# Where a head's sums get their start value, how the hashes are multiplied, and a list of jobs in another order

## The chip, the cores and the metric

The kernel runs on one core of one Trainium2 chip. The metric is the device time of one execution in microseconds (us); the lower the better. The core has a matrix engine (TensorE, PE in the profile, with its weight loads as PEld), VectorE (DVE), ScalarE (ACT), GpSimd (POOL) and SyncE (SP), each with a queue of its own that it works through in order, and 16 DMA engines that move data.

## What is computed

Attention over 4 batches of 8 heads, 768 tokens and 64 dimensions, in which a query sees only the keys of its own hash bucket, and behind it a layer that sends the 128 best tokens of a batch through a small network.

```python
q_bits = (einsum(q, proj) > 0)                 # 6 bits a token: its bucket; k_bits alike
mask   = q_bucket[..., :, None] == k_bucket[..., None, :]
scores = where(mask, q @ k.T / 8, -1e9)
attn   = softmax(scores)                       # sum + 1e-9 below
x      = (attn @ v) as (B, 768, 512)
# per batch: the 128 tokens with the highest x . w_gate
ye  = relu(xe @ w1) @ w2                       # 512 -> 1024 -> 512
out[top] = x[top] + sigmoid(x[top] . w_gate) * ye      # the other tokens keep x
```

## The kernel before

**The program is a list of words.** `ORDER` holds some 2,000 words such as `s.6.4`; `jobs` gives each its function, and the words are emitted one after the other. So each engine's queue is the list, filtered by engine: what stands ahead of an instruction on its engine has to be done first. `BANKS` deals the PSUM tiles (`big` 1024 columns, `one` 512) in the order in which they are asked for. The sums of a head have a PSUM bank of their own, the pool `pav` with one buffer, so that a head's sums can start only when those of the head before have been read.

**A head (0 to 31, eight to a batch) goes through these words.**
- `X` loads it (queries and keys transposed, float32), `xh` and `xl` split it into two float16 tiles XH and XL on ScalarE and GpSimd. `h` (line 342) multiplies four heads by the projection `pjt`, each in 32 columns of the array of its own (`tile_position`), `sg` takes the signs. `pa`, `pb`, `ps` are DMAs on SyncE's queue that put the parts into the operands A and B. Head 0 goes a shorter way (`hx`, `sx`, `da`, `dd`).
- `mx`, `re`, `rd` (lines 499, 507, 515): the largest bucket-matched score of a query, by differences of keys in three passes that ScalarE clamps between; `mt`, `mc`, `mr` (520, 524, 530) turn these maxima into a row and store it into A.
- `s.h.u` (565, 568): the scores in five units; `e` (581) the exponentials on ScalarE; `r` (595) their low halves on VectorE.
- `w` (606): the start value of the sums. It is what all the keys together give a query without a match: two products of 396 columns for each head, of a constant with `W`, which GpSimd makes from the sums of v (`vs`, `vw`).
- `a.h.c` (621): probabilities times values, 18 products of 64 or 65 columns for each of six chunks of keys. `rc` (631 to 633) and `n` (641) divide on VectorE; `po` stores.

**A batch** then scores its tokens (`sc`, `sl`), ranks them (`lt`, `ow`, counted by `cl`, `cw` on TensorE), makes the list (`se`, `ip`, `ix`), gathers the tokens (`ga`, GpSimd), and runs the network: `tx`, `hi`, `lo`, `up.b.f` (872, twelve products of 128 columns for each of eight f), `hh` and `hl` (the two halves of the hidden layer, ScalarE and VectorE), `dn.b.f` (903), `fi`, `sr` (scatter). For batches 0 to 2 this lies among the heads of the next batches; for batch 3 nothing comes behind it, and that is the tail of the program.

The lines that the steps turn on: `seed` 599 to 609, `hash_` 338 to 346, `load_pj` 252, `max_turn` 517 to 520, `finish` 907, `scatter` 914, and `ORDER`.

Of the kernel before, what the change touches and what calls it, by code (L numbers as in the profile page):

```python
# [45 lines left out]
w.0 pa.3.0 re.2.0.0 mx.1.0.2 pa.3.1 xl.2 re.2.1.0 rd.1.0 X.7 mx.2.0.1 xh.4 pb.1.2 mx.2.1.1 pb.1.3 re.2.0.1 vs.1 rd.1.1
rt.0 pa.4.0 re.2.1.1 X.6 rk.0.1 mx.2.0.2 rk.0.0 pb.2.3 ia.3 mt.1 mx.2.1.2 xh.5 rd.2.0 pb.2.2 s.0.0 pb.3.0 V.3 mc.1
pb.3.1 e.0.0 rd.2.1 s.0.2 mr.1 s.0.4 pa.4.1 e.0.2 mt.2 s.0.3 mc.2 vw.1 mr.2 s.0.1 e.0.3 r.0.0 ps.3.0 h.1.0.4 e.0.1
ia.4 ps.3.1 pb.4.0 e.0.4 a.0.0 sg.1.0.4 pa.5.0 a.0.1 pb.4.1 s.1.0 pa.5.1 ps.5.0 s.1.1 e.1.0 kd.3 ps.5.1 s.1.2 r.0.1
ps.4.0 e.1.1 mx.3.0.0 r.0.2 ps.4.1 mx.3.1.0 a.0.2 e.1.2 vs.2 a.0.3 re.3.0.0 a.0.4 a.0.5 r.1.0 re.3.1.0 s.1.3 rc.0 vs.3  # L50
# [922 lines left out]
```

## Time and profile before

| | us |
|---|---|
| median of 3 runs (lowest, highest) | 428.82 (427.92, 429.24) |
| the profiled execution's own time | 429.79 |
| its span, first to last instruction | 428.0 |
| busy in the span: TensorE | 388.4 |
| VectorE | 297.2 |
| ScalarE | 289.9 |
| GpSimd | 159.7 |

The profiled execution took 1.8 us more than its span, and 0.97 us more than the median. An engine's busy time counts each instant once, however many instructions overlap in it. TensorE's instructions overlap heavily: what one costs is read from the distance of two starts, not from its length.

### The profile page before, as it was taken

How to read it: one execution, taken by the hardware profiler on the slowest of the kernel's cores; microseconds unless marked ns; L12 is line 12 of the kernel's file. 1: busy time of each engine (PE TensorE's matmuls, PEld its weight loads, DVE VectorE, ACT ScalarE, POOL GpSimd, SP SyncE). 2: the span in 40 equal slices, each digit the busy share in tenths (PEclk: the TensorE clock that was granted, in tenths of full speed). 3: DMA queues.
4: the chain of work that ended last, by engine and by line, in shares of the span. 5: the costliest groups of instructions: out<-in, count | busy, mean ns of one | idle time of the engine just before them, and what ended most of it. 6: DMA issues, size and time to landing. Idle time of an engine off the chain costs nothing.

```text
span 428.0 us, 13488 instructions
## 1 busy us (share of the span) xinstructions
PE 388.4 (91%) x5633; PEld 291.0 (68%) x5640; DVE 297.2 (69%) x628; ACT 289.9 (68%) x367; POOL 159.7 (37%) x172
## 2 busy tenths in 40 slices
PE   0699999999989799999999999999999999999375
PEld 0255877777767577887667786887667777877272
DVE  1656767778786799767677978865859788467511
ACT  2677799698869877677857968678746877552010
POOL 9379668373726245414314150423141212000100
PEclk9759999999999999999999999999999999999679
DMA  8676268756484665514464257323343223001100
GB/s 242 195 192 160 63 182 252 242 167 165 107 289 88 157 176 184 159 53 124 110 190 142 66 149 229 86 59 99 105 128 96 64 61 100 2 3 71 54 2 25
DMA packets 33685, 53.87 MB, mean 126 GB/s; under 512 B 5726, under 2 KB 24920, under 8 KB 33624
## 3 DMA queue, kind: packets, MB, share of 16 engines
q1 hardware_dynamic: 22440, 33.48, 29.0%
q10 hardware_dynamic: 10544, 17.43, 12.9%
q0 software_dynamic: 640, 2.10, 1.6%
q8 instruction: 44, 0.72, 0.8%
q14 instruction: 17, 0.14, 0.1%
HBM read 25.78 MB, written 7.35 MB: 77 GB/s over the span
## 4 chain that ended last, share of the span: by engine, by line
PE 60%; DMA 12%; DVE 11%; issue 7%; SPq 5%; ACT 3%; ACTq 0%; POOL 0%; POOLq 0%; DVEq 0%
PE av L621 17%; PE mx L499 11%; PE s L565 10%; PE s L568 10%; DMA A<-XH 4%; PE hp L872 4%; DMA A<-sg 3%; PE yp L903 2%; DVE R L595 2%; PE av L606 2%; PE h L342 2%; DMA pjt<-in_pj_dram 2%; ACT mx L507 1%; DMA X<-in_qk_dram 1%; SPq L402 1%
## 5 line engine op out<-in xcount | busy, mean ns | idle before, releaser
L581 ACT ACTIVATE P<-s 128x1024 int32<-128x1024 f32 (+1 forms) x160 | 146.6, 938 | 45.8 <-PE s L568 43.2
L565 PE MATMUL s<-A 97*128 97x512 f16 (+1 forms) x384 | 118.3, 326 | 3.2 <-DVE mr L524 2.1
L507 ACT ACTIVATE mx<-mx 128x512 f32<-128x512 f32 (+2 forms) x127 | 100.2, 801 | 29.5 <-PE mx L499 23.7
L621 PEld LDWEIGHTS <-P 128*128 128x128 f16 x2304 | 114.6, 97 | 6.4 <-issue 0.6
L568 PE MATMUL s<-B 128*128 128x512 f16 (+1 forms) x384 | 118.0, 326 | 0.0
L621 PE MATMUL av<-V,P 128*128 128x65 f16 (+1 forms) x2304 | 118.0, 193 | 0.0
L621 PE MATMUL av<-VR,R 128*128 128x65 f16 x1152 | 114.6, 192 | 1.1 <-DVE R L595 1.1
L595 DVE TENSOR_SCALAR R<-P 128x1536 f16<-128x1536 uint16 x96 | 97.7, 1029 | 15.6 <-ACT P L581 15.5
L621 PEld LDWEIGHTS <-R 128*128 128x128 f16 x1152 | 105.2, 98 | 1.5 <-DVE R L595 1.5
L373 POOL TENSOR_TENSOR XL<-X,XH 128x768 f16<-128x768 f32 x32 | 53.5, 1677 | 86.3 <-DVE R L595 18.3
L515 DVE TENSOR_REDUCE m<-mx 128x2 f32<-128x512 f32 (+1 forms) x65 | 61.5, 951 | 20.0 <-PE mx L499 18.2
L499 PEld LDWEIGHTS <-A 96*128 96x128 f16 x570 | 53.6, 100 | 31.3 <-issue 12.2
L499 PE MATMUL mx<-kd,A 96*128 96x256 f16 (+1 forms) x378 | 63.0, 284 | 6.4 <-DVE kd L473 3.6
L568 PEld LDWEIGHTS <-B 128*128 128x128 f16 x384 | 37.6, 98 | 22.5 <-issue 3.9
L565 PEld LDWEIGHTS <-A 97*128 97x128 f16 x384 | 37.4, 97 | 19.3 <-issue 0.8
L499 PE MATMUL mx<-A 96*128 96x256 f16 (+1 forms) x192 | 33.2, 284 | 1.2 <-ACT mx L507 1.2
L444 POOL TENSOR_TENSOR vs<-Vf 128x384 f32<-128x384 f32 x16 | 17.9, 1122 | 42.2 <-DMA Vf<-in_v_dram 42.1
L915 POOL DMA_INDIRECT out_dram<-ye,idx x4 | 5.6, 1404 | 71.8 <-DVE ye L910 65.3
L362 ACT CAST XH<-X 128x768 f16<-128x768 f32 x32 | 26.5, 830 | 8.4 <-DMA A<-XH 5.9
L872 PE MATMUL hp<-xth,w1h 128*128 128x128 f16 x128 | 24.4, 229 | 2.3 <-DVE htl L890 0.9
L872 PE MATMUL hp<-xtl,w1h 128*128 128x128 f16 x128 | 24.3, 229 | 0.5 <-DVE ss L857 0.5
L473 DVE TENSOR_TENSOR kd<-A 96x512 f16<-96x512 f16 (+1 forms) x32 | 15.0, 471 | 14.0 <-PE mx L499 9.1
(97 smaller groups left out, 453.1 us busy)
## 6 DMA issues: line engine op xcount, KB each, us to landing
X<-in_qk_dram SPq DMA_DIRECT2D x30, 384.0 KB
Vf<-in_v_dram ACTq DMA_DIRECT2D x16, 384.0 KB
B<-A SPq DMA_DIRECT2D x64, 96.0 KB
B<-XL SPq DMA_DIRECT2D x64, 96.0 KB
out_dram<-x ACTq DMA_DIRECT2D x8, 768.0 KB
A<-XH SPq DMA_DIRECT2D x62, 96.0 KB
wt<-in_w_dram ACTq DMA_DIRECT2D x8, 512.0 KB
sbc<-scores SPq DMA_DIRECT2D x3, 384.0 KB
```

Of the source, the lines that this page charges most:

```text
L362: nc.scalar.copy(xh, st["X", h])
L373: turn(nc.gpsimd.tensor_tensor(**rest_x(h)))
L444: nc.gpsimd.tensor_tensor(y, t[:, 0:3], t[:, 3:6], op=ALU.add)
L499: nc.tensor.matmul(p[:, t - t0], a[0:96, 0, t * P : (t + 1) * P], keys, start=first, stop=True, skip_group_check=True,)
L507: nc.scalar.activation(p, p, AF.Relu)
L515: nc.vector.reduce_max(st["m", h][:, t0:t1], max_tile(h, g), axis=AX.X)
L565: nc.tensor.matmul(p[:, o : o + n], a[:, 1, c * P : (c + 1) * P], a[:, 0, q0 : q0 + n], start=True, stop=False,)
L568: nc.tensor.matmul(p[:, o : o + n], bt[:, 1, c * P : (c + 1) * P], bt[:, 0, q0 : q0 + n], start=False, stop=True,)
L581: nc.scalar.activation(pp[:, c0 : c0 + k, q0 : q0 + w], p[:, : k * w].rearrange("p (c q) -> p c q", c=k), AF.Exp, bias=PB * float(np.log(2 ...
L595: mine(nc.vector.tensor_scalar(r, pp.bitcast(U16)[:, :, 0::2], 2.0 ** -24, None, op0=ALU.mult,))
L621: nc.tensor.matmul(o[:, t, 0:n], l, r, start=False, stop=last and l is lo, skip_group_check=True,)
L872: nc.tensor.matmul(o, l[:, k, fs], st[r, b][:, xs], start=(f % 4 == 0 and k == 0 and i == 0), stop=(k == 3 and i == 2), skip_group_check=True,
```

## The change

- **The start value of the sums.** For each pair of heads TensorE makes one small product (`ws`, twice 132 columns), ScalarE copies it to SBUF (`wc`), and for each head ScalarE copies it, six times side by side, into the PSUM bank of the sums (`w`, 396 columns), in place of the two products of 396 columns. At the very start one product with zeros (`zb`) clears the bank.
- **The hash** of groups 1 to 7 is made from float16 pairs: projection high times XH, high times XL, low times XH, 24 products of 384 columns in place of 8 in float32. It then waits for XL, where it waited for X. `pp` makes the two halves of the projection.
- **The maxima** are clamped and rounded to float16 first (`mq`, VectorE), then turned in float16 (`mt`), then copied (`mc`).
- **The start.** The projection is loaded second on SyncE's queue, the other constants, the gate and the first weights later; the constant rows of A are written by VectorE and GpSimd in pieces; 30 products of a constant (`wu.0.30`) run ahead of the first hash; ScalarE's table is loaded by `it`.
- **The list.** It is made anew. All eight `up.2` now stand behind the last head's sums, with `dn.2`, `fi.2` and the scatter behind them; the scatter of batch 2 stands behind the gather of batch 3.
- **Buffers.** X 4 in place of 5, XH and XL 6 in place of 3; the rank's mask and the list's mask share a buffer; `fi` writes over its input.

```diff
 def seed(h):                                   # before; after: seed_act
-    for i in range(2):
-        nc.tensor.matmul(st["O", h], zs, w[:, i, h % 2].unsqueeze(1).broadcast_to([P, NC, OW]),
-                         start=(i == 0), stop=False, skip_group_check=True)
+def out_clear():
+    o = out_tile(0)
+    nc.tensor.matmul(o[:, : NC * OW], zs, zero, start=True, stop=True, skip_group_check=True)
+def sum_all(pr):
+    for i in range(2):
+        nc.tensor.matmul(
+            p[:, : 2 * OW], zs, W[pr % NV][:, i].rearrange("p h d -> p (h d)"), start=(i == 0), stop=(i == 1)
+        )
+def sum_copy(pr):
+    nc.scalar.copy(t.rearrange("p h d -> p (h d)"), st["wp", pr][:, : 2 * OW])
+def seed_args(h):
+    if h:
+        out_tile(h)
+    return st["O", h], st["W", h // 2][:, h % 2].unsqueeze(1).broadcast_to([P, NC, OW])
+def seed_act(h):
+    nc.scalar.copy(*seed_args(h))
...
 def hash_(g, j0, j1):
+        if g:
+            need(("pj",))
+            terms = ((pjh, "XH"), (pjh, "XL"), (pjl, "XH"))
+        else:
+            terms = ((pjt[:, 0:32], "X"),)
         for e in range(2):
-            for j in range(j0, j1):
-                nc.tensor.matmul(hp[32 * j : 32 * j + 32, ...], pjt[:, 0:32], st["X", 4 * g + j][...],
-                    start=True, stop=True, tile_position=(0, 32 * j))
+            for i, (w, x) in enumerate(terms):
+                for j in range(j0, j1):
+                    nc.tensor.matmul(hp[32 * j : 32 * j + 32, ...], w, st[x, 4 * g + j][...],
+                        start=(i == 0), stop=(i == len(terms) - 1), tile_position=(0, 32 * j))
...
+def max_clamp(h):
+    m = st["mq", h] = sb.tile([P, NC], F16, tag="mq", name=f"mq{h}", bufs=2)
+    nc.vector.tensor_scalar(m, st["m", h], FLOOR, 1.0 / MS, op0=ALU.max, op1=ALU.mult)
 def max_turn(h):
-    nc.tensor.transpose(out=p[:NC, :P], in_=st["m", h], identity=ident)
+    nc.tensor.transpose(out=p[:NC, :P], in_=st["mq", h], identity=ident16)
 def max_copy(h):
-    nc.vector.tensor_scalar(mr, st["mt", h][:NC, :P], FLOOR, 1.0 / MS, op0=ALU.max, op1=ALU.mult)
+    nc.vector.tensor_copy(mr, st["mt", h][:NC, :P])
...
 ORDER, behind the last head's products (two pieces):
-a.31.5 sc.3.1.3 dn.2.0 rc.31 dn.2.1 sl dn.2.2 n.31 dn.2.3 bp.0 po.7 dn.2.4 bc.0 bp.1 dn.2.5 ow.3.0 bc.1
+a.31.5 up.2.0 rc.31 up.2.4 sl up.2.5 n.31 up.2.1 po.7 bp.0 bp.1 bc.0 up.2.2 bc.1 ow.3.0 up.2.3 lt.3.0
```

How the instructions stand in the two programs follows at three places, as a listing of each queue prints it; a name's digits up to the underscore are its batch or head and part, those behind it only number the tile.

SyncE's queue at the start of the program, before (X0 and X1 are the first two heads, cs and c16 constants, pjt the projection):

```order
L298 DMA X0_96<-in_qk_dram 64x768
L298 DMA X1_103<-in_qk_dram 64x768
L256 DMA cs_67<-in_cst_dram 128x259
L253 DMA pjt_69<-in_pj_dram 128x96
L301 DMA X2_113<-in_qk_dram 128x768
L301 DMA X3_120<-in_qk_dram 128x768
```

And of the change:

```order
L321 DMA X0_103<-in_qk_dram 64x768
L262 DMA pjt_69<-in_pj_dram 128x99
L321 DMA X1_111<-in_qk_dram 64x768
L268 DMA c16_68<-in_cst16_dram 128x262
L324 DMA X3_120<-in_qk_dram 128x768
L324 DMA X2_155<-in_qk_dram 128x768
L432 DMA B0_87<-A0_82 64x768 x2
L422 DMA A1_83<-XH1_186 64x768 x2
```

The projection moved from the fourth place to the second, the float32 constants left this stretch.

TensorE at the seed of head 3 before: the last unit of its scores and the first of the two products of 396 columns, which stands there twice (zs is the constant, W1 the sums of v):

```order
L565 LDWEIGHTS A3_82
L565 MATMUL s3_4_1027<-A3_82 128x256
L568 LDWEIGHTS B3_87
L568 MATMUL s3_4_1027<-B3_87 128x256
L606 LDWEIGHTS zs_73
L606 MATMUL av3_1036<-W1_93,zs_73 128x396
```

And of the change ScalarE's queue around a seed, that of head 6 (P are exponentials, mx clamps, wp the small product, V a split of v, av the sums):

```order
L609 ACTIVATE P6_1_1803<-s6_3_1749 128x2x512
L537 ACTIVATE mx8_0_1739<-mx8_0_1739 128x1024
L647 COPY ws4_1846<-wp4_1830 128x132
L453 ACTIVATE V0_91<-Vf4_1115 128x12x64
L537 ACTIVATE mx8_1_1717<-mx8_1_1717 128x512
L656 COPY av6_1865<-ws3_1249 128x396
L609 ACTIVATE P6_1_1803<-s6_4_1835 128x2x256
L609 ACTIVATE P7_0_1890<-s7_0_1855 128x2x512
```

The start value left TensorE's queue and stands in ScalarE's, among instructions that wait for TensorE.

VectorE in the tail before, from the copy of the scores to the rank (co and cm are comparisons, ye the end of batch 2):

```order
L740 SCALAR_TENSOR_TENSOR co3_7799<-sbc3_7783,sc2_7771,cs_67 128x128
L703 COPY sbc3_7783<-bp_7784 128x384
L740 SCALAR_TENSOR_TENSOR co3_7799<-sbc3_7783,sc2_7771,cs_67 128x128 x2
L729 TENSOR_SCALAR cm3_0_7807,acc_74<-sbc3_7783,sc2_7771 128x640
L729 TENSOR_SCALAR cm3_2_7812,acc_74<-sbc3_7783,sc2_7771 128x384
L740 SCALAR_TENSOR_TENSOR co3_7799<-sbc3_7783,sc2_7771,cs_67 128x128
L910 SCALAR_TENSOR_TENSOR ye2_7821<-yp2_7759,ss2_7038,xe2_6954 128x512
L729 TENSOR_SCALAR cm3_1_7824,acc_74<-sbc3_7783,sc2_7771 128x512
L740 SCALAR_TENSOR_TENSOR co3_7799<-sbc3_7783,sc2_7771,cs_67 128x128 x2
L729 TENSOR_SCALAR cm3_4_7838,acc_74<-sbc3_7783,sc2_7771 128x128
L729 TENSOR_SCALAR cm3_3_7840,acc_74<-sbc3_7783,sc2_7771 128x256
L767 TENSOR_TENSOR rank3_7848<-rp3_7815,acc_74 128x6
```

And of the change:

```order
L753 COPY sbc3_7977<-bp_7978 128x384
L790 SCALAR_TENSOR_TENSOR co3_7999<-sbc3_7977,sc2_7946,cs_67 128x128
L779 TENSOR_SCALAR cm3_0_8013,acc_77<-sbc3_7977,sc2_7946 128x640
L779 TENSOR_SCALAR cm3_1_8015,acc_77<-sbc3_7977,sc2_7946 128x512
L790 SCALAR_TENSOR_TENSOR co3_7999<-sbc3_7977,sc2_7946,cs_67 128x128 x4
L779 TENSOR_SCALAR cm3_2_8060,acc_77<-sbc3_7977,sc2_7946 128x384
L779 TENSOR_SCALAR cm3_3_8062,acc_77<-sbc3_7977,sc2_7946 128x256
L790 SCALAR_TENSOR_TENSOR co3_7999<-sbc3_7977,sc2_7946,cs_67 128x128
L940 SCALAR_TENSOR_TENSOR htl2_8030<-hp2_7916,hth2_8029 128x512
L779 TENSOR_SCALAR cm3_4_8074,acc_77<-sbc3_7977,sc2_7946 128x128
L940 SCALAR_TENSOR_TENSOR htl2_8030<-hp2_7916,hth2_8029 128x512
L817 TENSOR_TENSOR rank3_8087<-rp3_8034,acc_77 128x6
```

Two instructions for the low half of batch 2's hidden layer (htl2) now stand ahead of the rank, and the end of batch 2 went behind it.

## Rows read from the trace of the kernel before

**Rows 1.** the page, busy time, share of the span and instructions of each engine

```profile
PE 388.4 (91%) x5633; PEld 291.0 (68%) x5640; DVE 297.2 (69%) x628; ACT 289.9 (68%) x367; POOL 159.7 (37%) x172
```

**Rows 2.** stretches of the span: length, busy time by engine, clock, DMA share, GB/s

```profile
0.00:32.60 32.60, 17.97 (x77) 9.09 (x78) 15.27 (x21) 18.09 (x24) 22.55 (x42) 0.79 0.72 210
32.60:157.00 124.40, 118.42 (x1774) 88.81 (x1774) 93.61 (x173) 104.10 (x130) 70.65 (x64) 1.00 0.60 167
157.00:390.20 233.20, 229.59 (x3606) 178.18 (x3609) 175.31 (x394) 165.31 (x210) 63.50 (x64) 1.00 0.38 106
390.20:428.00 37.80, 22.45 (x181) 14.92 (x179) 12.99 (x42) 2.36 (x5) 2.96 (x3) 0.80 0.12 42
```

**Rows 3.** timeline of TensorE near 164 us: start, length, engine, line, tiles, count

```profile
163.88 1.50 PE L342 MATMUL h<-X,pjt 128*32 128x384 f32 x16
165.31 0.39 PE L565 MATMUL s<-A 97*128 97x512 f16 x1
...
166.19 0.50 PE L606 MATMUL av<-W,zs 128*128 128x396 f16 x2
166.52 0.82 PE L499 MATMUL mx<-kd,A 96*128 96x256 f16 x6
```

**Rows 4.** timeline of TensorE near 94 us and 377 us, same columns

```profile
94.20 0.27 PE L520 MATMUL mt<-cs,m 128*6 128x128 f32 x1
94.30 0.60 PE L499 MATMUL mx<-kd,A 96*128 96x256 f16 x4
...
376.90 0.22 PE L872 MATMUL hp<-xth,w1h 128*128 128x128 f16 x1
...
377.57 0.50 PE L606 MATMUL av<-W,zs 128*128 128x396 f16 x2
```

**Rows 5.** groups of instructions by line and shape: busy us, mean ns | idle before

```profile
L507 ACT ACTIVATE mx<-mx 128x1024 f32<-128x1024 f32 x62 | 62.8, 1014 | 16.0 <-PE mx L499 13.5 <-DVE V L429 1.5 <-ACT XH L362 0.3
...
L342 PEld LDWEIGHTS h<-X,pjt 128*32 128x32 f32 x124 | 4.4, 111 | 15.1 <-issue 14.5 <-DMA X<-in_qk_dram 0.3
...
L703 ACT COPY sbc<-bp 128x384 f32<-128x384 f32 x1 | 0.5, 479 | 5.1 <-PE bp L696 5.1
```

**Rows 6.** timeline of VectorE behind a head's last product

```profile
163.98 0.17 DVE L631 TENSOR_SCALAR rc<-av 128x6 f32<-128x6 f32 x1 [0.21 <-PE av L621]
...
164.61 0.56 DVE L641 TENSOR_TENSOR x<-av,rc 128x384 f32<-128x384 f32 x1
```

**Rows 7.** timeline of the first 33 us, all engines

```profile
4.79 2.09 DVE L336 CAST A<-X 32x768 f16<-32x768 f32 x2 [4.79 <-DMA X<-in_qk_dram]
...
9.70 0.82 PE L342 MATMUL h<-X,pjt 128*32 128x384 f32 x1 [9.70 <-DMA pjt<-in_pj_dram]
...
18.28 1.44 PE L499 MATMUL mx<-kd,A 96*128 96x384 f16 x4 [3.63 <-DVE kd L473]
...
32.61 0.38 PE L565 MATMUL s<-A 97*128 97x512 f16 x1
```

**Rows 8.** timeline of the last 38 us: VectorE, GpSimd and TensorE

```profile
390.28 0.16 DVE L631 TENSOR_SCALAR rc<-av 128x6 f32<-128x6 f32 x1 [0.52 <-PE av L621]
...
399.95 0.17 DVE L767 TENSOR_TENSOR rank<-rp,acc 128x6 f32<-128x6 f32 x1 [0.42 <-PE rp L750]
...
401.93 0.98 POOL L786 DMA_INDIRECT xe<-out_dram,idx  x1 [2.98 <-DVE idx L781]
...
405.39 0.69 DVE L846 CUSTOM_DVE_ANT_0 jke<-xe,wgt 128x512 bf16<-128x512 f32 x1 [3.73 <-DMA xe<-out_dram,idx]
...
408.06 0.31 PE L872 MATMUL hp<-xth,w1l 128*128 128x128 f16 x1
408.17 0.31 PE L872 MATMUL hp<-xth,w1h 128*128 128x128 f16 x1
...
412.64 0.22 PE L872 MATMUL hp<-xth,w1h 128*128 128x128 f16 x1
...
415.33 0.69 DVE L890 SCALAR_TENSOR_TENSOR htl<-hp,hth 128x512 f16<-128x512 f32 x1 [7.13 <-PE hp L872]
```

More of the change, by code (lines that the diff above doesn't have):

```diff
@@ L46 @@
[L46 to L50, printed above, removed]
@@ L181, in consts @@
     least = np.where((p < 18) & (r >= 12) | (p >= 32) & (r < 6), -1.0, 0.0)
-    c = np.concatenate([ident, tiny, group[:, None], here[:, None], least[:, None]], axis=1).astype(np.float32)
+    c = np.concatenate([ident, tiny], axis=1).astype(np.float32)
+    s = np.stack([group, here, least], axis=1).astype(np.float32)
     iota = np.broadcast_to(p[None, :], (P, P))
     tok = np.arange(NC)[None, :] * P + p[:, None]
-    return np.ascontiguousarray(c), np.ascontiguousarray(np.concatenate([iota, tok], axis=1).astype(np.float16))
+    return c, s, np.ascontiguousarray(np.concatenate([ident, iota, tok], axis=1).astype(np.float16))
 @with_exitstack
@@ L313, in signs_direct @@
     def signs_direct(h, i):
-        need(("ia", h))
+        need(("ia", h, i))
         done("ps", h, i)
@@ L382, in place_signs @@
     def place_signs(h, i):
-        need(("sgd", h), ("ia", h % NA))
+        need(("sgd", h), ("ia", h % NA, i))
         free_a(h)
@@ L450, in v_sum2 @@
         if pr >= NV:
-            need(("as", 2 * (pr - NV) + 1))
+            need(("ws", pr - NV))
         done("w", pr)
@@ L532, in row_turn @@
     def row_turn(h):
-        need(*(("md", h, g) for g in range(len(groups(h)))))
-        p = st["mt", h] = big(f"mt{h}")
+        p = st["mt", h] = one(f"mt{h}").bitcast(F16)
         for t in range(NC):
-            nc.tensor.transpose(out=p[0:1, t * P : (t + 1) * P], in_=st["m", h][:, t : t + 1], identity=ident)
-    def row_clamp(h):
-        nc.vector.tensor_scalar(st["m", h], st["m", h], FLOOR, None, op0=ALU.max)
+            nc.tensor.transpose(
+                out=p[0:1, t * P : (t + 1) * P], in_=st["mq", h][:, t : t + 1], identity=ident16
+            )
     def row_copy(h, i):
         done("row", h, i)
-        q = slice(512 * i, min(512 * i + 512, S))
-        o, x = A[h][96:97, 0, q], st["mt", h][0:1, q]
-        if i:
-            nc.vector.tensor_scalar(o, x, 1.0 / MS, None, op0=ALU.mult)
-        else:
-            nc.scalar.activation(o, x, AF.Copy, scale=1.0 / MS)
+        q = slice(384 * i, 384 * i + 384)
+        (nc.vector.tensor_copy if i else nc.scalar.copy)(A[h][96:97, 0, q], st["mt", h][0:1, q])
     UNITS = (
@@ L560, in st_unit @@
     def st_unit(h, u):
-        need(*(("row", h, i) for i in (0, 1)), *(("pb", h, i) for i in range(4)))
+        need(("ia", h % NA, 2), *(("row", h, i) for i in (0, 1)), *(("pb", h, i) for i in range(4)))
         a, bt = A[h % NA], Bt[h % NBB]
```

354 lines of the change are left out of this document (190 added, 164 removed), and 6 rows, old and new, of the table BANKS.

## The prediction

> **What bounds the kernel now.** I read the busy times first. TensorE is busy 388.4 of 428.0 us, 91% [rows 1], no other engine more than 70%. That is a mean over unlike stretches, so I cut the span at the first score product, at head 11 and at the last sum [rows 2]. From 157.0 to 390.2 TensorE is busy 229.6 of 233.2 us with the clock at 1.00, the full 2.4 GHz: there an instruction taken off TensorE's queue shortens the program by what it occupied. From 32.6 to 157.0 it is 118.4 of 124.4, with ScalarE at 104.1, 84%. The first 32.6 us hold 18.0 us of it, the last 37.8 us 22.5. So the reader should see three things: a long middle bound by TensorE, with little slack on ScalarE in its first third; a start that waits for data; and a tail that is a chain through all engines. What an instruction occupies is the distance of two starts, since lengths overlap.
>
> **The change, part by part.**
>
> *Start values of the sums.* Two products of 396 columns run from 166.19 to 166.52 [rows 3], 0.33 us for a head, 32 heads: 10.6 us. In their place come 16 pairs of products of 132 columns. Twelve products of 128 columns take 0.67 us, from 376.90 to 377.57 [rows 4], 0.056 each, so 32 cost 1.8. TensorE gains 8.8 us. ScalarE gets 32 copies of 396 columns and 16 of 132. A copy of 384 took 479 ns [rows 5]; so the large ones are 0.49 each, the small ones between nothing and 0.48, of which I take half: 19.5 us in all, on an engine that was busy 289.9. It stays under TensorE, so I count no time for the sheer work.
>
> What it does cost is a hand-over. The sums have one bank. Before, once VectorE had read a head's sums, TensorE wrote the next start value itself. Now ScalarE has to, and behind its copy wait the exponentials that VectorE and TensorE need next. From the first division at 163.98 to the end of the normalising at 165.17 it is 1.19 us [rows 6]; with 0.49 for the copy 1.7, and I take 2.3 with the semaphores between, an estimate, since no row shows this chain. In this time TensorE needs other work. I added up, by the changed order and the spacings above (score products of 512 columns 0.22 each, four from 165.31 to 166.19 [rows 3]), what stands between the last product of a head's sums and the first of the next. The mean is 3.3 us; ten of 31 places have under 2.5, the third 1.3, and the last none at all: between heads 30 and 31 nothing is left to multiply, since `up.2` went into the tail. At 1.7 us a hand-over the shortfall sums to 2.1 us, at 2.3 to 3.9, and at 3.3, with one more ScalarE instruction of 1014 ns [rows 5] ahead of the copy, to 15.5. I take 4, half of it at head 31.
>
> *Hash.* A group of four heads runs from 163.88 to 165.31 [rows 3]: 1.43 us for 8 float32 products, which show as 16 pieces, 0.089 each. 384 columns once over at the spacing above are 0.165, so the float32 product makes two trips in each piece and four products share the array. 24 float16 products, four abreast, are 24 x 0.165 / 4 = 0.99. Seven groups gain 0.44 each: 3.1 us. That each waits for XL, from GpSimd, costs nothing where TensorE gets to it late; GpSimd is busy 37% [rows 1].
>
> The rule that speaks against this: the Trainium skill, "TensorEngine Tiling (Array Packing)", Restrictions under Tile-to-Partition Mapping, says that column tiling disables the fast weight load. The row agrees so far that these narrow loads last 111 ns on average [rows 5], but in float32 they were hidden under pieces of 89. By that rule 24 loads could be the limit; this is a rival below.
>
> *Maxima.* The turn runs from 94.20 to 94.30 [rows 4], 0.10; a float16 product of 128 columns is 0.056. 31 turns gain 1.5 us. `mq` adds a VectorE instruction on six columns to each head, ahead of a row that is due a head later: nothing.
>
> *Batch 2's network.* Eight `up.2` of 0.67 leave the stretch where TensorE is full: 5.4 us. In the tail they lie beside VectorE's scoring and ranking, where TensorE idles 15.4 of 37.8 us [rows 2].
>
> *Start.* The first product waited until 9.70 for the projection, while X0 was there at 4.79 [rows 7]. Now the projection is issued right behind half of X0. I let it land near 5 and 30 products of 128 columns run first, which at half clock take 30 x 0.107 = 3.2 us (spacing 408.06 to 408.17 [rows 8]) behind the memsets; so the first hash comes near 6.5, 3.2 us earlier. This is the lower end, if all else keeps its distance. The upper is the whole wait, 9.7. Between them I take 6: from 9.70 to the first maximum at 18.28 and the first score at 32.61 [rows 7] the chain goes through VectorE's signs and DMAs, and the new list puts head 0's signs first and two heads' maxima, not three, ahead of the first score. Against more stands ScalarE, which then has the splits, the weights and the exponentials at once. The float32 constants, the gate and the weights, moved behind, are used much later.
>
> *Tail.* From the division behind the last sum, 390.28, the rank comes at 399.95, the gather at 401.93, the tokens at 405.39 [rows 8]. Ahead of the rank VectorE now has two instructions of 0.69 [rows 8] in place of one like it: 0.7 later. On GpSimd the scatter of batch 2 goes behind the gather, which takes nothing from the path. On the other side, batch 3's first products stood 0.107 apart [rows 8], which is 1.2 GHz, after the idle time before them, and kept to it until 412.64, where their length falls from 0.31 to 0.22; that is 43 products, and at the full clock they save 43 x 0.051 = 2.2. Now `dn.2` runs until shortly ahead of them. I take 1.0 gain, between 0.7 lost and 2.5 gained.
>
> The clock is read from rows here. The Trainium skill, "TensorE: Matmul & The Clock Gate", Part 1, says that the clock follows how busy the array has been lately; the trace agrees (0.80 in the tail, 1.00 in the middle [rows 2]). By that rule the tail gains the whole 2.2 if `dn.2` runs close enough ahead, and none if the gather's wait is too long for it.
>
> *Buffers and the rest*: nothing; each shared buffer's readers and writers follow each other on one engine or lie far apart.
>
> **Sum.** On TensorE 8.8 + 3.1 + 1.5 + 5.4 = 18.8 off; hand-overs 4 on; start 6 off; tail 1 off: 21.8. The profiled execution took 429.79, so 408.0, and with the 0.97 by which the median lies lower 407.0.
>
> **Rivals.**
> - *Every hand-over waits behind a ScalarE instruction*: 15.5 in place of 4, so 418.5. For it: ScalarE at 84% in the first third, plus the copies. Against: from 157 on it is at 165.3 of 233.2, 71%.
> - *The hash is bound by its weight loads*: 24 x 0.111 = 2.66 us a group, 1.23 more than before where I counted 0.44 less: 7 x 1.67 = 11.7 us, so 419. For it: the 111 ns; against: loads of 111 ns came every 89 ns before, so they overlap one another too.
> - *The new list also closes the holes of the first heads*: 6.0 us of idle TensorE between 32.6 and 157.0 [rows 2], so 401. For it: XH and XL have six buffers, so loads run further ahead. Against: ScalarE is fuller there.
> - *Slower*: the hand-over between the heads takes over as the bound, since the copy stands behind two exponentials and the exponentials behind it: 4.3 us each. The shortfall sums to 34.7 over the 31 places, so 437.7. It decides from 3.9 us a hand-over on, where the shortfall passes 25.8 and the gain is gone. Against: it needs two full waits of ScalarE at nearly every head, while 289.9 and 19.5 us of work leave it a quarter of the time free.
>
> **How the numbers follow.** A measurement of this kernel can tell about 0.3% from no change, 1.3 us. My forecast has 0.66, waits behind ScalarE 0.13, weight loads 0.06, closed holes 0.10, slower 0.05. The first four are faster; a mishap of two of them together reaches the old time, so faster 0.92, same 0.03, slower 0.05. The forecast alone: firm TensorE 18.8, hand-overs 2 to 8, start 3.2 to 9.7, tail 0.7 lost to 2.5 gained, so 400 to 415. The range takes in three rivals: 397 to 420.
>
> **What would show it.** In the profile after: the products at the seeds gone and 32 copies of about 0.49 us on ScalarE; a hash group near 1.0 us and not 1.4 or 2.7; the first hash near 6.5 and the first score before 28; the last sum near 369, with a hole of some 2 us ahead of head 31; the last network's first products 0.056 apart. I am wrong if TensorE's idle time in the middle grows by much more than 4 us, with sums waiting for ScalarE's copy, or if the first score comes no earlier than 30.

## The result, and the profile after

The changed kernel takes 426.37 us (median of 9 runs, 424.21 to 427.07) against 429.24 (9 runs, 427.92 to 432.02): a ratio of 0.9919, 95% interval 0.9895 to 0.9944. It is faster by 0.8%, 2.9 us, where the forecast was 22. Each row below is from one profiled execution of its kernel; the changed one's took 425.49.

The first line of the page answers to [rows 1]:

```profile
PE 386.1 (91%) x5695; PEld 287.6 (68%) x5695; DVE 301.2 (71%) x671; ACT 306.1 (72%) x416; POOL 144.7 (34%) x163
```

TensorE is as full as before. The new cut of the span shows more. I took the same three marks in both kernels: the end of head 0's normalising, that of head 4's, and the first division behind the last sum. Columns as in [rows 2]. First the kernel before:

```profile
0.00:46.20 46.20, 31.56 (x257) 18.14 (x258) 23.89 (x34) 27.85 (x35) 33.98 (x55) 0.85 0.65 184
46.20:88.00 41.80, 41.51 (x633) 31.45 (x631) 31.39 (x60) 36.65 (x46) 25.35 (x20) 1.00 0.67 200
88.00:390.30 302.30, 293.01 (x4568) 226.49 (x4573) 228.93 (x493) 223.00 (x283) 97.37 (x95) 1.00 0.42 117
390.30:428.00 37.70, 22.35 (x179) 14.92 (x179) 12.97 (x42) 2.36 (x5) 2.96 (x3) 0.80 0.12 42
```

Then the changed one:

```profile
0.00:41.40 41.40, 30.79 (x261) 19.20 (x262) 29.66 (x43) 28.15 (x39) 29.30 (x49) 0.84 0.76 213
41.40:93.90 52.50, 45.13 (x674) 32.64 (x672) 35.91 (x72) 43.61 (x58) 28.84 (x27) 1.00 0.65 191
93.90:385.50 291.60, 282.61 (x4489) 216.70 (x4489) 221.55 (x513) 230.81 (x314) 83.67 (x86) 1.00 0.41 115
385.50:423.70 38.20, 27.59 (x277) 19.11 (x273) 14.09 (x44) 3.55 (x7) 2.94 (x3) 0.88 0.12 42
```

The second row of each is the result. Heads 1 to 4 took 41.8 us, with TensorE idle 0.3; now they take 52.5, with 7.4 idle and 3.6 more busy. What the start had won, 4.8, is lost twice over: head 4 ends 5.9 us later. Most of the 4.8 was borrowed, too: by head 0's end the old list has 44 score products and two groups of hashes behind it, the new one 28 and one, with the maxima level (59 products and 63). These 16 products and the group are some 3.6 us by their spacings; by head 4's end the two are level again. From there to the last sum 10.7 us are won; the tail is 0.4 longer, from the divisions at 390.28 [rows 8] and 385.56 on.

The steps that the prediction named, in the changed kernel's timeline: the first hash, the first maximum, the first score (the start rows answer to [rows 7]); a hash group and a turn (to [rows 3, 4]).

```profile
6.48 1.95 PE L330 MATMUL hx<-X,pjt 128*32 128x384 f32 x6
...
14.41 0.97 PE L529 MATMUL mx<-kd,A 96*128 96x384 f16 x4 [3.95 <-DVE kd L503]
...
24.44 0.59 PE L593 MATMUL s<-A 97*128 97x512 f16 x1 [0.94 <-ACT A L576]
...
47.61 0.35 PE L371 MATMUL h<-XH,pjh 128*32 128x384 f16 x4
...
48.42 0.35 PE L371 MATMUL h<-XH,pjl 128*32 128x384 f16 x4
...
202.92 0.27 PE L596 MATMUL s<-B 128*128 128x256 f16 x1
203.13 0.22 PE L554 MATMUL mt<-c,mq 128*6 128x128 f16 x1
203.28 0.61 PE L529 MATMUL mx<-kd,A 96*128 96x256 f16 x4
```

The hash starts at 6.48 and a group takes six steps of 0.163, 0.98 us: both as forecast. The first score comes at 24.44, 8.2 earlier. The turn is not as forecast. The product ahead of it should hold the array 0.11, but the turn starts 0.21 behind it, and the next product 0.15 behind the turn: 0.24 us for a float16 turn, where the float32 one took 0.10 to 0.11 with nothing ahead of it [rows 4]. In 27 of 31 heads the next product stands 0.15 behind the turn.

The groups of the added instructions, by line and shape:

```profile
L656 ACT COPY av<-ws 128x396 f32<-128x396 f32 x32 | 16.0, 501 | 5.1 <-DVE x L691 5.0
L647 ACT COPY ws<-wp 128x132 f32<-128x132 f32 x16 | 4.3, 271 | 0.8 <-PE wp L641 0.8
```

20.3 us on ScalarE, where I had 19.5. Behind VectorE's normalising the copies ended, on average over 31 heads, 2.9 us after the last product of the head before had started; TensorE waited for one of them alone, the last:

```profile
382.04 0.22 PE L671 MATMUL av<-V,P 128*128 128x65 f16 x2 [1.87 <-ACT av L656]
```

Now ScalarE and TensorE near 90 us, in the stretch that was lost (timelines; ACTq is an issue from ScalarE's queue):

```profile
84.36 1.53 ACT L609 ACTIVATE P<-s 128x1024 int32<-128x1024 f32 x2
88.74 0.38 ACTq L441 DMA_DIRECT2D Vf<-in_v_dram  x1
89.17 1.94 ACT L609 ACTIVATE P<-s 128x1024 int32<-128x1024 f32 x2 [3.28 <-DMA B<-XL]
```

```profile
90.24 0.38 PE L593 MATMUL s<-A 97*128 97x512 f16 x1 [0.57 <-ACT P L609]
...
93.00 0.60 PE L529 MATMUL mx<-kd,A 96*128 96x256 f16 x4 [0.96 <-ACT mx L537]
```

The exponential at 89.17 does not read B. In front of it in ScalarE's queue stands an issue, the load of V, that goes out at 88.74 and by the program's order waits for a semaphore of an earlier transfer and for VectorE. While the issue waits, ScalarE does nothing for 3.28 us, and TensorE then waits for ScalarE. The same happens at 44.25 (2.11 us, a weight's issue), and TensorE waits 1.19 at 45.68. At 75.15 a weight split waits 1.93 us for its transfer; the clamps stand behind it in ScalarE's queue, and TensorE's longest wait of the stretch follows:

```profile
75.15 1.04 ACT L861 CAST w1h<-wt 128x1024 f16<-128x1024 f32 x1 [1.93 <-DMA wt<-in_w_dram]
76.10 1.49 ACT L537 ACTIVATE mx<-mx 128x1024 f32<-128x1024 f32 x2
...
77.16 0.86 PE L529 MATMUL mx<-A 96*128 96x256 f16 x6 [2.63 <-ACT mx L537]
```

These four waits, 1.19, 2.63, 0.57 and 0.96, are 5.4 of the 7.4 us.

The tail, lines that answer to [rows 8]:

```profile
385.56 0.17 DVE L681 TENSOR_SCALAR rc<-av 128x6 f32<-128x6 f32 x1 [1.40 <-PE av L671]
...
395.74 0.15 DVE L817 TENSOR_TENSOR rank<-rp,acc 128x6 f32<-128x6 f32 x1
...
398.34 0.96 POOL L836 DMA_INDIRECT xe<-out_dram,idx  x1 [53.86 <-DVE idx L831]
...
401.84 0.68 DVE L896 CUSTOM_DVE_ANT_0 jke<-xe,wgt 128x512 bf16<-128x512 f32 x1
```

From the division to the rank 10.18 us, before 9.67; to the gather 12.78, before 11.65. The last network starts at 2.4 GHz, but from 404 on its products stand 0.10 to 0.11 apart again; in the two stretches from 404 to 408 the granted clock is 0.51 and 0.64. This depends on the execution. Fourteen profiles of this case have the new tail (here and in the experiments): in seven the clock stayed at 1.00 from the division until the last network was done, and the tail took 35.4 to 35.9; two took 36.1 and 36.4; in five, this one among them, it fell twice, and they took 37.7 to 38.2. The old tail's six profiles had it at 0.50 for 8 us each and took 36.8 to 38.3. The tail of the changed kernel with the turns back in float32, last of the experiments, is one that kept the clock; columns as above:

```profile
386.00:421.90 35.90, 25.16 (x275) 17.33 (x273) 14.08 (x44) 3.55 (x7) 2.94 (x3) 0.97 0.13 45
```

### The profile page after: what moved, and what is told of

It reads as the page before. It is cut to its first block, busy times and chain, and to the rows that moved or that the text cites. A ratio compares the mean times of both kernels' runs of the same rounds, so it can differ in the third digit from the quotient of the medians.

```text
span 423.7 us, 13639 instructions
## 1 busy us (share of the span) xinstructions
PE 386.1 (91%) x5695; PEld 287.6 (68%) x5695; DVE 301.2 (71%) x671; ACT 306.1 (72%) x416; POOL 144.7 (34%) x163
## 4 chain that ended last, share of the span: by engine, by line
PE 39%; DMA 7%; DVE 6%; issue 5%; SPq 2%; ACT 1%; POOLq 0%; POOL 0%; DVEq 0%; ACTq 0%
PE av L671 12%; PE s L593 6%; PE s L596 6%; PE mx L529 5%; PE yp L953 4%; PE hp L922 3%; DMA xe<-out_dram,idx 2%; DMA sbc<-scores 2%; DMA A<-XH 1%; DVE cm L779 1%; DMA A<-mr 1%; DVE R L623 1%; DVE m L545 1%; DVE co L790 1%; DMA out_dram<-xe,idx 1%
## 5 line engine op out<-in xcount | busy, mean ns | idle before, releaser
L609 ACT ACTIVATE P<-s 128x1024 int32<-128x1024 f32 (+1 forms) x160 | 146.0, 941 | 36.2 <-PE s L596 29.7
L671 PE MATMUL av<-V,P 128*128 128x65 f16 (+1 forms) x2304 | 119.2, 193 | 2.0 <-ACT av L656 1.9
L537 ACT ACTIVATE mx<-mx 128x512 f32<-128x512 f32 (+2 forms) x127 | 99.1, 801 | 18.8 <-PE mx L529 16.8
L623 DVE TENSOR_SCALAR R<-P 128x1536 f16<-128x1536 uint16 x96 | 95.1, 1002 | 19.0 <-ACT P L609 17.6
L403 POOL TENSOR_TENSOR XL<-X,XH 128x768 f16<-128x768 f32 x30 | 49.2, 1644 | 106.2 <-DVE rc L681 46.3
L545 DVE TENSOR_REDUCE m<-mx 128x2 f32<-128x512 f32 (+2 forms) x65 | 61.2, 951 | 27.2 <-PE mx L529 24.6
L529 PEld LDWEIGHTS <-A 96*128 96x128 f16 x570 | 52.0, 99 | 31.7 <-issue 16.5
L529 PE MATMUL mx<-kd,A 96*128 96x256 f16 (+1 forms) x378 | 60.7, 279 | 7.6 <-DVE kd L503 4.0
L593 PEld LDWEIGHTS <-A 97*128 97x128 f16 x384 | 37.7, 98 | 22.1 <-DMA A<-mr 2.4
L529 PE MATMUL mx<-A 96*128 96x256 f16 (+1 forms) x192 | 32.0, 284 | 3.2 <-ACT mx L537 3.1
L836 POOL DMA_INDIRECT xe<-out_dram,idx x4 | 5.1, 1279 | 70.3 <-DVE idx L831 70.2
L922 PE MATMUL hp<-xth,w1l 128*128 128x128 f16 x128 | 23.8, 227 | 0.0
```

The source lines that it names most:

```text
L403: turn(nc.gpsimd.tensor_tensor(**rest_x(h)))
L529: nc.tensor.matmul(p[:, t - t0], a[0:96, 0, t * P : (t + 1) * P], keys, start=first, stop=True, skip_group_check=True,)
L537: nc.scalar.activation(p, p, AF.Relu)
L545: nc.vector.reduce_max(st["m", h][:, t0:t1], max_tile(h, g), axis=AX.X)
L593: nc.tensor.matmul(p[:, o : o + n], a[:, 1, c * P : (c + 1) * P], a[:, 0, q0 : q0 + n], start=True, stop=False,)
L609: nc.scalar.activation(pp[:, c0 : c0 + k, q0 : q0 + w], p[:, : k * w].rearrange("p (c q) -> p c q", c=k), AF.Exp, bias=PB * float(np.log(2 ...
```

## The experiments

Ratios are to the kernel before, timed anew in each round (428.1 to 429.9), with 95% intervals. "Head 4" is the end of its normalising: 88.0 before, 93.9 changed.

**Seeds on VectorE; ScalarE relieved.**

```diff
-w.0 ... w.31
+wd.0 ... wd.31
```

> The changed kernel with the 32 copies of start values on VectorE instead of ScalarE, at the same places of the list. Theory (ScalarE, over 90% busy from 32 to 157 us, has become a second bound of the first third, so that TensorE waits for its clamps): 6 us leave ScalarE in heads 0 to 11 and 10 later; TensorE's waits for the clamps shrink, the normalising of head 11 ends 3 to 5 us earlier than 168.9, the time falls from 426.4 to 421 to 423. Rival (late transfers and the new order of the list, not ScalarE's load): 425.5 to 427. Rival (a hand-over at each head): the hole ahead of head 31 shrinks from 2.0 to about 1 us and 1 to 2 us go, heads 1 to 11 as they were.

429.88 us, 1.0006 (0.9976 to 1.0037): slower than the changed kernel. TensorE waits 7.3 us for the copies, 11 times: VectorE's queue is the worse place.

```diff
-wh.0 wh.1 wh.3 xh.5 xh.6 xh.7 xh.8 xh.10 xh.11
+wv.0 wv.1 wv.3 xd.5 xd.6 xd.7 xd.8 xd.10 xd.11
```

> The changed kernel with three weight splits (1.05 us each) and six splits of X (0.84 us each) that ScalarE did between 33 and 80 us on VectorE instead: 8.2 us less for ScalarE there, and nothing else moved. Theory (ScalarE's load bounds heads 1 to 4): the normalising of head 4 ends 4 to 6 us earlier than 93.4 and the time is 421 to 423. Rival (transfers come late: TensorE and ScalarE wait for a weight at 75 and for the low halves of X at 44 and 89): head 4 within 1.5 us of 93.4 and 425.5 to 427.

425.99, 0.9938 (0.9912 to 0.9963), no different from the changed kernel; head 4 ends at 95.0. ScalarE's load is not the bound of heads 1 to 4.

**One part alone in the old list.**

```diff
+ws.k wc.k   (k = 0 to 15, about a dozen words ahead of the pair's first seed)
 def seed(h):
+    if h: nc.scalar.copy(st["O", h], ...); return
```

> The kernel before with one part of the change alone: the start values of heads 1 to 31 by ScalarE's copies, out of 16 small pairs of products, each placed where the list has the seed. By the terms of the prediction: 8.8 us off TensorE, 2 to 4 us of hand-overs on, so 423 to 425 against 429.2. Theory (ScalarE's load counts in the first third): of the first 12 heads' 3.3 us nothing stays, so 425 to 427. Rival (a hand-over behind a ScalarE instruction at every head): the whole gain is gone, 429 or more.

442.35, 1.0300 (1.0261 to 1.0339). The copies alone, in the old list, cost 13 us. This was my rival on the slow side, at 4.3 us a hand-over. But the trace has a hand-over of 3.4 us on average, and two stops like the one above:

```profile
129.68 0.35 ACTq L412 DMA_DIRECT2D Vf<-in_v_dram  x1
130.13 0.58 ACT L508 ACTIVATE mx<-mx 128x512 f32<-128x512 f32 x1 [4.88 <-DMA out_dram<-x]
...
276.50 0.36 ACTq L412 DMA_DIRECT2D Vf<-in_v_dram  x1
276.91 0.60 ACT L582 ACTIVATE P<-s 128x512 int32<-128x512 f32 x1 [3.67 <-DMA A<-sg]
```

```diff
-X.0 ia.1 X.1 lg lc V.0 lp V.1
+X.0 lp ia.1 X.1 lc V.0 lg V.1
```

> The kernel before with its projection loaded right behind the first half of X0 and the float32 constants and the gate behind it; nothing else. By the prediction the first hash starts 3 us earlier (near 6.5 instead of 9.7) and these 3 us are there at the end: 426. Theory (the first heads are set by what ScalarE and the transfers do until 90 us, not by the first hash): the first score comes up to 3 us earlier, head 4 at most 1 us, and the time is 428 to 430.

429.30, 1.0005 (0.9978 to 1.0032). The first hash came earlier (7.81) and nothing was won. The profiled execution, the fastest of twelve, kept the clock at 1.00 through the start, had its first maximum 1.75 earlier and ended 3.2 us earlier; the median did not. The move is not quite the projection's alone: ScalarE's issues shifted with it, and its first casts came at 7.76 instead of 9.42.

**Issues off ScalarE's queue.** In both kernels, and in the one with the copies alone:

```diff
 def load_v / load_w / load_gate / put_out:
-    nc.scalar.dma_start(...)
+    nc.sync.dma_start(...)
```

> The changed kernel with the loads of V, of the weights and of the gate and the stores of the output issued by SyncE instead of ScalarE, at the same places of the list. Theory (an issue on ScalarE's queue that waits for a free buffer or for an earlier transfer holds up the exponentials and clamps behind it: ScalarE stood idle 2.1 us before the weights' issue at 44.3 and 3.3 us before V's issue at 88.7, and TensorE waited for ScalarE right behind each): these stops go, the normalising of head 4 ends 4 to 6 us earlier than 93.9, the time is 420 to 423. Rival (the wait only moves to SyncE's queue and holds up the rows of A and B behind it): head 4 within 2 us of 93.9 and 425 to 428.

> The kernel before with the same edit: loads of V, the weights and the gate and the stores of the output issued by SyncE. Theory: ScalarE stood idle around such an issue for 1.3, 1.5, 3.0 and 1.8 us at 85, 104, 125 and 221 us, but TensorE lost little of it there; 1 to 3 us, so 426 to 428. Rival: 429 or more, since the start's loads of V then queue behind X.

> The kernel before with the start values by ScalarE's copies (442.4 as measured) and with the loads and stores issued by SyncE. Theory (most of the 13 us that the copies cost in the old list is the hand-over itself, 3.4 us from the last product to the copy's end with too little to multiply in it, and a part is ScalarE stopped by issues, 4.9 us at 130 and 3.7 at 277): 435 to 439. Rival (all of it is ScalarE stopped by issues): below 430. Rival (none of it): 441 or more.

Changed kernel: 425.14, 0.9899 (0.9861 to 0.9938), not clear of its 0.9919 without the edit; head 4 at 91.6, 2.3 us earlier, less than expected. TensorE's idle time in heads 1 to 4 fell to 3.9, but they still take 51.4: a new wait of 1.54 for a row of maxima stands at 50.50, and from 48 to 56 the clock fell (0.85 and 0.73 in the two stretches of 4 us), which cost up to 1.7 us, an estimate from these two numbers. Kernel before: **422.40, 0.9828 (0.9794 to 0.9861)**: this edit alone beats the whole change. With the copies: 429.86, 0.9985 (0.9947 to 1.0023), 12.5 us better than with ScalarE issuing. With SyncE's issues the copies cost 7.5 us (429.86 against 422.40), with ScalarE's 13.3 (442.35 against 429.05): so by these medians some 5.8 of the 13.3 come through ScalarE's stopped queue. The rest fits the hand-over: from head 0 to the last sum TensorE is idle 8.0 us more than without the copies, 7.5 of them in 14 waits for a copy, and busy 4.0 less (profiled executions, 4.1 us apart). Of what the kernel before gains, a part lies at the start. ScalarE's first instructions in the kernel before, then with the issues moved:

```profile
7.76 0.33 ACTq L796 DMA_DIRECT2D wt<-in_w_dram  x1
8.12 1.28 ACT L332 ACT_TABLE_LOAD   x1 [8.12 <-DMA X<-in_qk_dram]
9.42 1.67 ACT L332 CAST A<-X 32x768 f16<-32x768 f32 x2
```

```profile
1.99 1.28 ACT L332 ACT_TABLE_LOAD   x1 [1.99 <-issue]
3.98 1.68 ACT L332 CAST A<-X 32x768 f16<-32x768 f32 x2 [0.71 <-DMA X<-in_qk_dram]
```

In the old start the projection and ScalarE behind its issues ended nearly together. The hash was done near 14.2 us; what VectorE has to do ahead of the signs, the low half of V, waited for ScalarE and ended at 14.51:

```profile
13.46 1.05 DVE L429 SCALAR_TENSOR_TENSOR V<-Vf,V 128x768 f16<-128x768 f32 x1 [6.57 <-ACT V L423]
14.54 1.01 DVE L354 TENSOR_SCALAR sg<-h,cs 32x768 f16<-32x768 f32 x1
```

With the casts 5.4 us earlier, the first maximum came at 15.80 instead of 18.28. Head 0 ended 4.6 and head 11 7.3 earlier, but the issues did not do that alone, since the clock differs. From 16 to 30 us, in the kernel before, with the projection first, and with the issues on SyncE:

```profile
16.00:30.00 14.00, 10.81 (x42) 5.82 (x43) 8.52 (x14) 8.35 (x11) 6.69 (x7) 0.52 0.56 148
16.00:30.00 14.00, 10.64 (x70) 6.54 (x71) 10.66 (x17) 11.76 (x16) 9.45 (x11) 1.00 0.69 178
16.00:30.00 14.00, 11.81 (x71) 7.23 (x70) 9.96 (x16) 12.10 (x17) 10.15 (x12) 0.88 0.75 215
```

Against the second, which kept the clock, moving the issues brought head 0 1.6 us forward (43.18 to 41.60) and head 11 5.7 (163.59 to 157.90): by that measure more than half of the gain lies behind the start. How much of the clock is owed to the moved issues, and how much to the execution, is open.

**The new list without the copies.**

```diff
 def seed_act(h):
-    nc.scalar.copy(*seed_args(h))
+    for i in range(2): nc.tensor.matmul(st["O", h], zs, W[...][:, i, h % 2]...)
```

> The changed kernel and its list, but with the start values written by TensorE again (two products of 396 columns a head at the place of the copy), so without the copies and the 16 small products; all other parts of the change stay. By the terms of the prediction TensorE gets 8.8 us more and the hand-overs' 2 to 4 us go: 431 to 433. Theory (the copies also press on a full ScalarE queue in the first third, where the new list loses 10 us): 426 to 429, the hole ahead of head 31 under 0.5 us. Rival (the copies bring nothing even in the new list): 423 to 426.

429.06, 1.0007 (0.9977 to 1.0038). So the copies bring 2.7 us in the new list by the medians (3.8 by the ratios), and all the rest of the change together nothing. Head 4 is late here too (95.7; up to 3.4 us of it a fallen clock, 0.64 and 0.59 near 48 and 80): the copies are not what heads 1 to 4 lose by.

**What heads 1 to 4 lose by** (both on the changed kernel with SyncE's issues).

```diff
-wt.0 ... wl.0.1 ... wt.1 ...   (four weights in heads 0 to 4)
+one weight a head, heads 3 to 11
```

> The changed kernel with its loads and stores issued by SyncE (425.1), and in its list the loading and splitting of the eight weight pieces spread over heads 3 to 11, one a head, instead of four of them in heads 0 to 4. Theory A (what the new list loses in heads 1 to 4 is crowding: the DMA engines, GpSimd and ScalarE do the weights there besides the splits): head 4 ends 3 to 5 us earlier than 91.6 and the time is 421 to 423. Theory B (it is a chain: only two heads' maxima are done ahead of the first score, so TensorE waits for clamps and rows that are not ahead): head 4 within 1.5 us of 91.6, 424 to 426.

468.30, 1.0963 (1.0906 to 1.1021). TensorE waited 15.6 us for rows of the maxima; GpSimd's halves of the weights now stood ahead of the low halves of X. As a time it tells what a wrong place costs. But of these waits all except 1.9 us lie behind head 4. In heads 1 to 4 only one weight is left, split from 80.7 us on. This stretch, so relieved, and then as it was with SyncE's issues:

```profile
39.20:90.60 51.40, 47.56 (x684) 34.33 (x683) 36.63 (x72) 43.24 (x57) 24.71 (x21) 0.97 0.51 145
40.20:91.60 51.40, 47.50 (x680) 33.65 (x678) 37.21 (x72) 45.07 (x59) 29.73 (x27) 0.97 0.67 199
```

The DMA engines were busy 0.51 instead of 0.67, GpSimd 24.7 us instead of 29.7, and the stretch took the same 51.4: crowding by the weights (theory A) is out.

```diff
-... s.0.0 pa.2.0 mx.1.0.2 ... mx.2.0.0 ...
+pa.2.0 mx.1.0.2 rd.1.0 kd.2 mx.2.0.0 ... rd.2.1 s.0.0 ...
```

> The changed kernel with its loads and stores issued by SyncE (425.1), and in its list the maxima of head 2 ahead of the first score, as the kernel before had them, and no other move. Theory B (the early first score is no gain: it comes by leaving work for later that then stands in a chain): the first score comes 3 us later, but head 4 ends 2 to 4 us earlier than 91.6; 421.5 to 423.5. Theory A (crowding by transfers and splits): head 4 no earlier than 91.6; 425 to 428.

433.07, 1.0117 (1.0064 to 1.0169): head 0 ends 6.4 us later than with SyncE's issues alone and head 4 6.3 later; heads 1 to 4 take 51.4 again. Theory B falls.

```diff
 (the edits of the relieved ScalarE and of SyncE's issues together)
```

> The changed kernel with its loads and stores issued by SyncE (425.1) and with three weight splits and six splits of X moved from ScalarE to VectorE, 8.2 us between 33 and 80 us. With ScalarE's queue no longer stopped by issues, the theory of its load gets its fair test: if the load counts in heads 1 to 4, head 4 ends 3 us or more earlier than 91.6 and the time is 421 to 423. Rival (the load never counted): 424 to 426.

423.37, 0.9881 (0.9836 to 0.9927), head 4 at 91.7 as without the relief, with the clock at 1.00 in heads 1 to 4, which take 50.8. ScalarE's load is out.

```diff
-mx.0.0.0
+wu.1.60 mx.0.0.0
```

> The changed kernel (426.4) with 60 more products of 128 columns whose result nobody reads, put in TensorE's queue between the first hashes and the first maxima, where it stands idle from 10.4 to 14.4 us. Theory (that idle stretch lets the clock fall to 1.2 GHz from 15.5 to 28.5 us, which costs up to 5 us of product time): the clock stays at 2.4 GHz beyond 20 us, head 0 ends 2 to 4 us earlier than 41.4, the time is 422 to 424.5. Rival (the start is a chain through the other engines and the clock is not what limits it): head 0 within 1 us and 425.5 to 427.5.

426.01, 0.9874 (0.9812 to 0.9935); two of its six runs, 420.3 (at a mean granted clock of 0.989, the highest) and 422.6, lay well below the others (426.0 to 427.1). In the profiled one, 426.64, the clock did stay at 1.00 until 20 us, head 0 ended 1.2 earlier, and head 4 ended later, at 95.2 (up to 1.7 us of it a fallen clock, 0.75 and 0.83 from 76 to 84). The clock of the start is not what heads 1 to 4 lose by.

**Terms by themselves, in the old list with SyncE's issues.**

```diff
-X.0 ia.1 X.1 lg lc V.0 lp
+X.0 lp ia.1 X.1 lc V.0   (lg comes some 60 words later)
```

> The kernel before with its loads and stores issued by SyncE (422.4), with the projection right behind the first halves of X0 and X1 and the gate later. By the prediction's step on the start the first hash moves from 8.8 to about 7 and that stays: 420.5. Theory (the start is set by ScalarE's splits and the chain through signs, not by the first hash): 421.5 to 423.

422.37, 0.9887 (0.9835 to 0.9939): the projection's place is worth nothing here either.

```diff
-... up.2.0 mt.30 up.2.4 ... a.31.5 sc.3.1.3 dn.2.0 rc.31 ...
+... mt.30 ... a.31.5 sc.3.1.3 up.2.0 rc.31 up.2.4 sl ...   (the changed tail)
```

> The kernel before with its loads and stores issued by SyncE (422.4), and batch 2's first layer moved out of heads 28 to 31 behind the last sum, with the changed kernel's order of the tail; nothing else of the change. The prediction's terms: eight pieces of 0.67 us leave the full stretch, the select comes 0.7 later: last sum 5.4 us earlier, 417 to 418.5. Rival (the freed time is lost again, since head 31's start value and the exponentials of heads 30 and 31 then come last): 420 or more.

417.68, 0.9759 (0.9710 to 0.9808). In the profiles the last sum comes 5.1 us earlier than without the move (378.62 against 383.70) and the tail is 1.1 longer, in one of the executions in which the clock fell there. This term was right.

```diff
 (on the version just above)
-mx.0.1.0
+wu.20 mx.0.1.0
```

> The kernel before with loads and stores issued by SyncE and batch 2's first layer in the tail (417.7), with 20 products of 128 columns that nobody reads between the first hashes and the first maxima. Theory of the clock: its fall from 22 to 25.5 us goes or comes later, 416 to 417.3. Rival: 417.5 to 419.

**414.73, 0.9657 (0.9605 to 0.9709)**, the best version: faster than both kernels. What the 20 products add is not shown: its interval ends where that of the version above begins, the six runs of each overlap (412.4 to 417.7 and 415.5 to 420.4), and the granted clock still fell between 20 and 28 us in the profiled execution.

```diff
 (on the 417.68 version)
-h.g on X in float32
+h.g on XH, XL for g = 3 to 7; xl and xh of the group moved ahead of it
```

> The kernel before with loads and stores issued by SyncE and batch 2's first layer in the tail (417.7), with the hashes of groups 3 to 7 from float16 pairs, whose low halves GpSimd makes up to one head earlier for it. The prediction's term: five groups at 0.44 us, so 415 to 416. Rival (the earlier low halves hold up something else): 417.5 or more.

418.86, 0.9746 (0.9687 to 0.9804): no gain. In the profiles the groups are 0.98 us long, yet the last sum comes only 0.2 earlier. The edit also moved the splits of X, so whether these took back what the hash gave is open.

**The turns back in float32**, in the changed kernel and on its relieved form with SyncE's issues:

```diff
-p = one(...).bitcast(F16); transpose(..., identity=ident16)
+p = one(...); transpose(..., identity=ident)     (heads 4 to 31)
```

> The changed kernel (426.4) with the turns of the maxima of heads 4 to 31 in float32 again; the clamp ahead of the turn stays. In the trace of the changed kernel the product behind a float16 turn starts 0.15 us later, and the turn starts 0.09 later than the product before it would let it, 0.24 in all; in float32 it was 0.11 with nothing ahead of it. Theory (the float16 turn costs TensorE 0.13 us more, not 0.05 less): 28 turns, 3.6 us, so 422.5 to 424. The prediction's term (a float16 turn is 0.05 shorter): 1.4 us more, 427.5 to 428.

> The changed kernel with loads and stores issued by SyncE and ScalarE relieved of nine splits (423.4), with the turns of heads 4 to 31 in float32 again. Theory: 3.6 us less, 419 to 421. Prediction's term: 424.5 or more.

426.06, 0.9957 (0.9924 to 0.9991), and 423.25, 0.9884 (0.9841 to 0.9926): by the medians 0.3 and 0.1 us less than their partners, by the ratios 0.4% more and the same, so no difference. The price on TensorE went; a row of the first one's timeline:

```profile
131.15 0.38 PE L597 MATMUL s<-B 128*128 128x512 f16 x1
131.37 0.27 PE L555 MATMUL mt<-cs,mq 128*6 128x128 f32 x1
131.48 0.60 PE L529 MATMUL mx<-kd,A 96*128 96x256 f16 x4
```

3.6 us came off TensorE and next to nothing off the time.

## Why the prediction was wrong

The step that failed is **Start**, with its condition "if all else keeps its distance". I let 6 us of the start reach the end. By my terms head 4 would have ended at 88.0 - 6 - 1.4 (five seeds) - 0.9 (two hashes) = 79.7; it ended at 93.9. These 14.2 us are most of the 16.6 by which the last sum missed 369; behind head 4 my terms had 13.0 and 10.7 came. Two things were wrong in it.

First, what held the old start. I took the wait for the projection, 9.70 [rows 7], as the chain's first link, because it was the longest wait of TensorE. Moving the projection alone gave nothing in the time, twice (429.30; 422.37 against 422.40). ScalarE's work from the casts at 9.42 on, behind issues that waited, was a second link, 0.3 us later at the signs; taking the issues away brought the first maximum 2.5 us forward, and with a higher clock head 0 4.6.

Second, the new list's heads 1 to 4, for which I had no term at all. I read the stretch from 32.6 on as bound by TensorE and let the new order keep that. It did not: 7.4 us idle where there had been 0.3, and 3.6 more busy. Of the idle time 5.4 us follow three stops of ScalarE, two at its own issues and one at a weight's landing. With the issues moved head 4 came 2.3 us earlier, half of that already at head 0; the idle time fell to 3.9, and the fallen clock may hide a part. Heads 1 to 4 took 50.8 to 55.0 us in every version of the new list that I tried, and 41 to 45 in every one of the old: so the copies, ScalarE's load, the third head's maxima, the weights and the clock of the start are not the cause by themselves. Left, with the issues moved, are some ten waits of 0.1 to 1.5 us for exponentials, clamps, low halves and a row of maxima; whether another order would have these ahead is open. The early first score misled: it came 8.2 us earlier, but with 26 products of maxima behind it instead of 48, and by head 0's end some 3.6 us of scores and hashes were still owed.

*Seeds and hand-overs.* The counts held: 0.50 us a copy, and by their spacings 8.5 us of seeds, 3.1 of hashes and 5.4 of batch 2's layer gone from TensorE ahead of the last sum. The hand-over was 2.9 where I took 2.3, and the hole ahead of head 31 2.03 where I took 2. In the new list that price is small, as forecast. The rival on the slow side was real in the old list: 442.35. I had priced it with a hand-over of 4.3 and the new list's places; the run shows 3.4, with ScalarE stopped by issues on top.

*ScalarE's 19.5 us at nothing.* Right for its load. What I did not see is that its queue also carries issues, and an issue that waits stops it. The row that told it stood in the trace before: ScalarE idle 3.04 us ahead of a clamp, with an issue at its end:

```profile
124.65 0.35 ACTq L411 DMA_DIRECT2D Vf<-in_v_dram  x1
125.10 0.58 ACT L507 ACTIVATE mx<-mx 128x512 f32<-128x512 f32 x1 [3.04 <-DVE sc L667]
```

The Trainium skill, "TensorE: Matmul & The Clock Gate", Part 1, "Architectural detail: the array is 16× 32×32, not 1× 128×128", calls ScalarE's queue a strict FIFO; these rows agree.

*Hash.* Mechanism and size right, 0.98 a group; the rival of weight loads is out. The Trainium skill's rule that column tiling disables the fast weight load ("TensorEngine Tiling (Array Packing)", Restrictions) did not make the time: the 95 ns loads lie under one another. But in the old list the gain did not reach the end.

*Turns.* Wrong sign: 0.24 instead of 0.056, a loss of 0.13 each where I had a gain of 0.05. It hardly mattered, since undoing it brought 0.1 to 0.3 us. The premise of the prediction's first paragraph, that in the middle an instruction off TensorE shortens the program by what it occupied, did not hold for what is small and spread over the heads. Turns (3.6 us) gave 0.3 at most, hashes (2.2, with splits moved for them) nothing, the copies (8.5 of TensorE less 2 for the hole) 2.7. The one block of 5.4 us near the end gave 4.7.

*Batch 2's network.* Right. *Tail.* Forecast 1.0 gained, in the profiled execution 0.4 lost: the select came 0.5 later as forecast (0.7), the gather 0.6 on top, and the clock fell again at 404 in spite of the products ahead. In the seven profiles that kept the clock the gather came 12.1 to 12.2 us after the division, 0.5 later than before, and the tail was shorter than any old one. Over all of them the new tails took 36.5 on average (14 profiles), the old ones 37.5 (6): the 1.0 that I forecast, but from two forms and not from one, and with which of them a run takes I had nothing to say.

## What to carry to other kernels

When a list is written anew, follow the first heads up to where the pipeline is full, and compare both kernels at marks that have the same products behind them: an early first score that leaves work for later is no gain. Before pricing work that goes to an engine, look at what else its queue carries: a transfer's issue that waits for a buffer or for an earlier transfer stops everything behind it, and the profile books the wait under the next instruction's name. A term of many small savings on a full engine is an upper bound; a block taken off the end of a full stretch was worth most of what it occupied. And one profile is one execution: before a stretch is credited to an edit, compare its granted clock in both.

## What the runs showed of the hardware that was not expected

- A float16 turn of 128 columns held TensorE 0.24 us, 0.09 ahead of it and 0.15 to the next start; a float32 one 0.10 to 0.11 in all. In the profile the float16 one looks shorter, 0.22 against 0.27.
- Which queue issues the loads was worth 1.7% in the kernel before (422.40 against 429.87) and 12.5 us with the copies in it.
- The same tail took 35.4 to 35.9 us with the granted clock at 1.00 and 37.7 to 38.2 where it fell twice, in different executions.
- Copies of 396 columns out of a tile that repeats six times took 501 ns on ScalarE, and copies of 132 columns 271.
